# A Strassen identity for half of an output projection, with partial products accumulated on copied PSUM banks

## The chip, the cores and the metric

One core of one Trainium2 chip runs the whole kernel in one launch. The metric is the device time of one execution in microseconds (us); lower is better.

Engines in the profile: PE is the matrix engine (TensorE), PEld its weight loads, DVE is VectorE, ACT is ScalarE, POOL is GpSimd, SP issues most DMAs (289 of 348 in the profile before).

## The reference, cut to what matters

```python
xn = layernorm(x)                                  # 2048 tokens x 1024
q, k, v = split(xn @ wqkv)                         # 32 heads of 32
pq, pk = phi(q), phi(k)                            # phi(t) = (t+1 if t>0 else exp(t)) + 1e-6
kv, z  = einsum("bhsd,bhse->bhde", pk, v), sum(pk)
o = (pq @ kv) / (pq @ z + 1e-6)                    # linear attention
s = o @ wo                                         # <- the projection that is changed
g = silu((silu(xn @ w_gate) * (xn @ w_up)) @ w_down)
return x + s * g
```

Everything is bf16 at the borders; D = 1024, F = 3584.

## The kernel before

It has three stages. Stage 1 makes k, v and their products over all tokens. Stage 2 makes q, o and s for four blocks (0 to 3) of 512 tokens. Stage 3 is the gated MLP, already done with a Strassen identity; its weights are prepared ahead of time: ScalarE squares a weight piece to get a bound, VectorE scales it by a power of two, GpSimd forms four differences (T1 to T4). These "preparation steps" run inside stages 1 and 2.

Stage 2, cut:

```python
def emit_phi(work, t_ps, dst, W, in_place=False, act=False):
    if act:                                            # blocks 1 to 3
        nc.scalar.activation(out=e_t, in_=t_ps, func=ACT.Relu, scale=-1.0)
        nc.scalar.activation(out=e_t, in_=e_t, func=ACT.Exp, scale=-1.0)
        nc.scalar.activation(out=t_ps, in_=t_ps, func=ACT.Relu)
        nc.vector.scalar_tensor_tensor(out=dst, in0=e_t, scalar=EPS, in1=t_ps, ...)   # pqT
        return
    ...
def emit_ND(b, t, nd):            # numerator and denominator of one 128-token tile
    for g in range(G):            # 8 matmuls of 128x132 into three PSUM banks
        nc.tensor.matmul(nd[:, j, gi, :], lhsT=pqT[:, g, ttok], rhs=KVZ[:, g, :], ...)
    ...                           # VectorE: rden = 1/(den + EPS), then o_sb = num * rden
def emit_OT(b, t):                # o transposed by DMA; two oT buffers
    nc.sync.dma_start_transpose(out=oT_tiles[b][:, :, t*P:(t+1)*P], in_=o_blks[b][:, t, :])
def emit_S(b, t, cc):             # half a row tile of s: 8 matmuls of 128x512
    for c in range(G):
        nc.tensor.matmul(s_ps, lhsT=oT[:, c, ttok], rhs=wo_sb[:, c, cc*CW:(cc+1)*CW], ...)
    nc.scalar.copy(out=s_sb[...], in_=s_ps)
    ...
for b in range(NB):               # block b: q of b+1 mixed with s of b-1, nd of b in between
    q  = [q_item(b + 1, g) for g in range(G)] if b + 1 < NB else []
    sl = sh(b - 1, 0) + sh(b - 1, 1) if b > 0 else []
    ...                           # each nd_item also does one preparation step for b > 0
emit_Ssum(passes[0])              # VectorE: four 128x2048 sums S1 to S4 for stage 3
```

Of the kernel before, what the change touches and what calls it, by code (L numbers as in the profile page):

```python
# [21 lines left out]
def kernel(  # L22
# [41 lines left out]
    LEAD = 6  # L64
    NPK = 8

    wqkv_v = A_wqkv.rearrange("(dc p) n -> p dc n", p=P)
# [31 lines left out]
    nc.vector.memset(ones[:], 1.0)  # L99
    mask = persist.tile([P, P], FP32, name="mask")  # L100
    nc.vector.memset(mask[:], 0.0)
    for j in range(HPG):
        nc.vector.memset(mask[j * DH:(j + 1) * DH, j * DH:(j + 1) * DH], 1.0)
    sel = persist.tile([P, HPG], FP32, name="sel")
    nc.vector.memset(sel[:], 0.0)
# [13 lines left out]
    late = p12.enter_context(tc.tile_pool(name="late", bufs=1, reuse_waits="tile"))  # L119
    v_bufs = [late.tile([P, G, NDW], BF16, name=f"v_sb{k}") for k in range(2)]  # L120
    for k in range(2):
        nc.gpsimd.memset(v_bufs[k][:, :, P:P + 1], 1.0)
    KVZ = late.tile([P, G, NDW], BF16, name="KVZ")
# [3 lines left out]
    pk_drams = {}  # L127
    rc_all = persist.tile([P, 3 * NFG], FP32, name="rc_all")
    cs_all = persist.tile([P, 3 * NFG], FP32, name="cs_all")
    lam = persist.tile([P, NFG], FP32, name="lam")  # L130
    rcl = persist.tile([P, NFG], FP32, name="rcl")
    hsc = persist.tile([P, 3], FP32, name="hsc")
    chs, rch, hmx = hsc[:, 0:1], hsc[:, 1:2], hsc[:, 2:3]

    def emit_phi(work, t_ps, dst, W, in_place=False, act=False):
        e_t = work.tile([P, W], FP32, name="e_t", tag="e_t")
        if act:
            nc.scalar.activation(out=e_t[:], in_=t_ps, func=ACT.Relu, scale=-1.0)
            nc.scalar.activation(out=e_t[:], in_=e_t[:], func=ACT.Exp, scale=-1.0)
            nc.scalar.activation(out=t_ps, in_=t_ps, func=ACT.Relu)  # L140
            nc.vector.scalar_tensor_tensor(out=dst, in0=e_t[:], scalar=EPS, in1=t_ps,
                                           op0=ALU.add, op1=ALU.add)
            return
        nc.scalar.activation(out=e_t[:], in_=t_ps, func=ACT.Exp)
        if in_place:
            r = t_ps
            nc.vector.tensor_scalar(out=r, in0=t_ps, scalar1=0.0, scalar2=EPS, op0=ALU.max, op1=ALU.add)  # L147
        else:
            r_t = work.tile([P, W], FP32, name="r_t", tag="r_t")
            r = r_t[:]  # L150
            nc.scalar.activation(out=r, in_=t_ps, func=ACT.Relu)
            nc.vector.tensor_scalar(out=r, in0=r, scalar1=EPS, scalar2=None, op0=ALU.add)
        nc.vector.scalar_tensor_tensor(out=dst, in0=e_t[:], scalar=1.0, in1=r,  # L153
                                       op0=ALU.min, op1=ALU.add)
# [7 lines left out]

    def emit_Q(b, g):
        if b not in pqT_tiles:
            pqT_tiles[b] = blk12.tile([P, G, TB], BF16, name="pqT", tag="pqT")
        pqT = pqT_tiles[b]
        btok = slice(b * TB, (b + 1) * TB)
        q_ps = ps2.tile([P, TB], FP32, name="q_ps", tag="B2")
        for dc in range(DC):
            nc.tensor.matmul(q_ps[:], lhsT=wq_sb[:, dc, g * P:(g + 1) * P], rhs=xn_ap(dc, btok),  # L170
                             start=(dc == 0), stop=(dc == DC - 1))
        emit_phi(phiw, q_ps[:], pqT[:, g, :], TB, in_place=True, act=b > 0)

# [79 lines left out]

    def emit_st2(key, t, later=False):
        tot = stp.tile([P, 1], I32, name="tot", tag="tot")
        nc.vector.tensor_scalar(out=tot[:], in0=st_tiles.pop(key).bitcast(I32), scalar1=1, scalar2=0x3f800000,
                                op0=ALU.logical_shift_right, op1=ALU.bitwise_and)
        c = kcol(key)
        ri, ci = rc_all[:, c:c + 1].bitcast(I32), cs_all[:, c:c + 1].bitcast(I32)
        nc.vector.tensor_scalar(out=ri, in0=tot[:], scalar1=52 << 23, scalar2=None, op0=ALU.add)  # L260
        nc.vector.tensor_scalar(out=ci, in0=ri, scalar1=-1, scalar2=254 << 23, op0=ALU.mult, op1=ALU.add)
        if not later:
            emit_sc(key, t)
# [84 lines left out]
    with ExitStack() as p1:  # L348
# [4 lines left out]

        wkv_sb = wpool.tile([P, DC, 2 * D], BF16, name="wkv_sb")

        p1_man = ExitStack()
# [218 lines left out]
        emit_Bev(1, 3)  # L575
        emit_C(0)
        for i in range(2, NT):
            for c in range(NCH):
                if (i, c) != (2, 0):
                    emit_Bmm(i, c)  # L580
# [4 lines left out]
                emit_Bev(i, c)  # L585
                if c == 3 and i in (4, 6, 7):
                    prep(1)
# [15 lines left out]
        for j in range(NJ):  # L603
# [5 lines left out]
                                    in0=kvz_ps[:, j, 0:ng, P:P + 1].to_broadcast([P, ng, HPG]),  # L609
                                    in1=sel[:, None, :].to_broadcast([P, ng, HPG]), op=ALU.mult)  # L610
        for g in range(1, G):
            emit_Q(0, g)
            if g == 3:
                prep(1)
        p1_man.close()

    p2_man = ExitStack()
    p2_man.enter_context(tc.manual_schedule(engines={mybir.EngineType.SP}))
    s_sums = {}

    def emit_Ssum(p):
        x1 = xn_blk_tiles[2 * p]
# [4 lines left out]
        S4 = a21.bitcast(F16)  # L627
        nc.vector.tensor_tensor(out=S1[:], in0=a21, in1=a22, op=ALU.add)
        nc.vector.tensor_tensor(out=S2[:], in0=S1[:], in1=a11, op=ALU.subtract)
        nc.vector.tensor_tensor(out=S3[:], in0=a11, in1=a21, op=ALU.subtract)  # L630
        nc.vector.tensor_tensor(out=S4, in0=a12, in1=S2[:], op=ALU.subtract)
        s_sums[p] = (S1, S2, S3, S4, a22)

    with ExitStack() as p2:
        otp = p2.enter_context(tc.tile_pool(name="p2oT", bufs=2, reuse_waits="tile"))
        work = p2.enter_context(tc.tile_pool(name="p2work", bufs=4, reuse_waits="tile"))
        small = p2.enter_context(tc.tile_pool(name="p2small", bufs=6, reuse_waits="tile"))
        blk_es = ExitStack()
        blk = blk_es.enter_context(tc.tile_pool(name="p2blk", bufs=2, reuse_waits="tile"))
        oT_tiles = {}  # L640
# [3 lines left out]
        def emit_ND(b, t, nd):  # L644
            pqT = pqT_tiles[b]
            ttok = slice(t * P, (t + 1) * P)
            if b not in o_blks:
                o_blks[b] = blk.tile([P, TPB, D], BF16, name="o_blk", tag="o_blk")
            o_sb = o_blks[b][:, t, :]
            for g in range(G):  # L650
# [4 lines left out]
            for j0, j1, ng in ((0, NJ - 1, GPT), (NJ - 1, NJ, G - (NJ - 1) * GPT)):  # L655
                nc.vector.tensor_scalar(
                    out=rden[:, j0 * GPT:(j1 - 1) * GPT + ng, :].rearrange("p (j g) h -> p j g h", j=j1 - j0),
                    in0=nd[:, j0:j1, 0:ng, P:P + HPG], scalar1=EPS, scalar2=None, op0=ALU.add)
            nc.vector.reciprocal(out=rden[:, 0:G, :], in_=rden[:, 0:G, :])
# [9 lines left out]
        def emit_OT(b, t):  # L669
            if t == 0:  # L670
                oT_tiles[b] = otp.tile([P, G, TB], BF16, name="oT", tag="oT")
            nc.sync.dma_start_transpose(out=oT_tiles[b][:, :, t * P:(t + 1) * P], in_=o_blks[b][:, t, :])

        def emit_S(b, t, cc):
            oT = oT_tiles[b]
# [3 lines left out]
            s_sb = s_tiles[(b, t)]  # L679
            s_ps = ps2.tile([P, CW], FP32, name="s_ps", tag="B2")  # L680
            for c in range(G):
                mm = nc.tensor.matmul(s_ps[:], lhsT=oT[:, c, ttok], rhs=wo_sb[:, c, cc * CW:(cc + 1) * CW],  # L682
                                      start=(c == 0), stop=(c == G - 1))
                marks.setdefault(("S", b, t), mm)
            nc.scalar.copy(out=s_sb[:, cc * CW:(cc + 1) * CW], in_=s_ps[:])  # L685
            if cc == NCC - 1:
                r0 = b * TB + t * P
                nc.scalar.dma_start(out=s_dram[r0:r0 + P, :], in_=s_tiles.pop((b, t))[:])

        def q_item(b, g):  # L690
            return lambda: emit_Q(b, g)
# [4 lines left out]
        def nd_item(b, t):  # L696
            def f():
                raw, nd = psa_tile("nd")

                def nd_ot():  # L700
                    emit_ND(b, t, nd)
                    emit_OT(b, t)
                if b > 0 and (b < NB - 1 or t % 2 == 0):
                    stat_ps[0] = lambda: raw[:, 0, 511:512]
# [13 lines left out]

        for b in range(NB):
            q = [q_item(b + 1, g) for g in range(G)] if b + 1 < NB else []  # L720
            sl = sh(b - 1, 0) + sh(b - 1, 1) if b > 0 else []
            body = q[:2] + mix(q[2:], sl)
            at = (1, 4, 7, 10) if len(body) > 12 else ((1, 3, 5, 7) if b == 0 else (0, 2, 4, 6))
            for k, f in enumerate(body):
                f()
                if k in at:
                    nd_item(b, at.index(k))()
        b = NB - 1
        blk_es.close()
        blk12_es.close()  # L730
        sp = ctx.enter_context(tc.tile_pool(name="p3S", bufs=1, side="right", reuse_waits="tile"))
        emit_Ssum(passes[0])
        stat_ps[0] = lambda: psa_tile("st_ps3")[0][:, 0, 511:512]
        prep_flush()
        nc.scalar.preload_act_table(ACT.Silu)
        for f in sh(b, 0) + sh(b, 1):
            f()
    p2_man.close()
# [511 lines left out]
```

## Time and profile before

| | before |
|---|---|
| median of the first three runs | 764.8 us (764.25 to 765.98) |
| first q matmul, first matmul of stage 3, first of the last down projections | 127.83, 249.69, 748.80 us |
| stage 1 (first k·v product to first q), stage 2, stage 3 up to that point | 102.63, 121.86, 499.11 us |

The marks are start times of the first matmul of that kind in the timeline. First the busy times on the page (busy us, share of the span, instructions):

```profile
PE 752.7 (99%) x3731; PEld 350.4 (46%) x3731; DVE 543.6 (71%) x1026; ACT 348.3 (46%) x479; POOL 269.1 (35%) x382
```

TensorE bounds the kernel: only 9 us of 762.1 are not matmul time. Second, stage 2 in the table of stretches; after the stretch's length come busy us of PE, PEld, DVE, ACT and POOL, each with its instruction count, the granted PE clock, the DMA share and GB/s.

```profile
127.00:166.00 39.00, 36.62 (x206) 17.56 (x205) 29.30 (x65) 26.62 (x46) 20.94 (x18) 1.00 0.65 191
166.00:210.00 44.00, 44.00 (x246) 21.51 (x245) 29.46 (x82) 38.86 (x62) 26.86 (x24) 1.00 0.98 269
210.00:262.00 52.00, 52.00 (x275) 24.90 (x274) 29.40 (x62) 24.48 (x39) 19.43 (x17) 1.00 0.89 278
```

From 166 us on PE is full. VectorE has room throughout (29 of 39, 29 of 44, 29 of 52), ScalarE except in the middle stretch (39 of 44), and GpSimd is busy for half of the time (67 of 135 us in the sum of that table). This invites moving work off PE. Third, what PE waited for (total us, times, longest), as far as it concerns stage 2:

```profile
PE nd L652 <- DVE o_blk L663: 1.7, 2, 1.2
...
PE nd L652 <- DVE pqT L153: 0.4, 1, 0.4
...
PE q_ps L170 <- DVE pqT L153: 0.2, 1, 0.2
```

Together 2.3 us. In the timeline the sums S1 to S4 of stage 3 take 2.15, 2.06, 1.21 and 1.23 us. These are the sums S1 to S4 of stage 3 in the timeline (start, us, engine, line, operation, out<-in, shapes), with the GpSimd instruction that ran at the same time:

```profile
236.30 2.15 DVE L628 TENSOR_TENSOR S<-xnT 128x2048 f16<-128x2048 bf16 x1
...
237.33 2.13 POOL L283 TENSOR_TENSOR w_sb<-w_sb 128x512 f16<-128x512 bf16 x1
...
238.49 2.06 DVE L629 TENSOR_TENSOR S<-S,xnT 128x2048 f16<-128x2048 f16 x1
...
240.47 1.21 DVE L630 TENSOR_TENSOR S<-xnT 128x2048 f16<-128x2048 bf16 x1
...
241.72 1.23 DVE L631 TENSOR_TENSOR xnT<-xnT,S 128x2048 f16<-128x2048 bf16 x1
```

Four instructions of one size and kind take 2.15, 2.06, 1.21 and 1.23 us. The two slow ones ran while GpSimd was at work, and the GpSimd instruction next to them took 2.13 instead of its usual 1.15 us.

### The profile page before, as it was taken

Reading aid. Unit: us, or ns where it says so; the run is one execution under the profiler, and the core shown is the slowest. Engines: PE = TensorE matmul, PEld = TensorE weight load, DVE = VectorE, ACT = ScalarE, POOL = GpSimd, SP = SyncE. Lnnn points to the kernel's source line nnn. Section 1 sums busy time; section 2 is a strip of 40 time slices with the busy share of each in tenths; the row PEclk is TensorE's granted clock in tenths of the full one; section 3 lists DMA queues with packets and bytes.
Section 4 is the critical chain, followed back from the end, with each engine's and each line's share of the span. In section 5 each row is a group of like instructions: output and inputs, shape, how many; then the busy total and the mean of one; then the engine's idle time right before and its main releaser. Section 6 shows DMA issues by size and latency. Waiting matters only on the chain.

```text
span 762.1 us, 10455 instructions
## 1 busy us (share of the span) xinstructions
PE 752.7 (99%) x3731; PEld 350.4 (46%) x3731; DVE 543.6 (71%) x1026; ACT 348.3 (46%) x479; POOL 269.1 (35%) x382
## 2 busy tenths in 40 slices
PE   8999999999999999999999999999999999999997
PEld 3444444444444444444444444444444444444444
DVE  7788676876656588888889885358676767787335
ACT  4545777688853566666448411132323222211022
POOL 0577699708563255868655000110000000200000
PEclk9999999999999999999999999999999999999999
DMA  9986799669889769897887237398654445530824
GB/s 315 302 151 125 204 298 319 248 139 286 238 263 263 250 231 308 290 359 289 314 310 281 86 86 260 116 355 329 228 190 177 166 165 170 170 144 15 281 81 136
DMA packets 105908, 170.29 MB, mean 223 GB/s; under 512 B 34688, under 2 KB 82176, under 8 KB 95232
## 3 DMA queue, kind: packets, MB, share of 16 engines
q1 hardware_dynamic: 99280, 143.81, 59.9%
q0 software_dynamic: 3984, 21.24, 7.0%
q10 hardware_dynamic: 2592, 4.59, 1.8%
q8 instruction: 29, 0.48, 0.3%
q14 instruction: 23, 0.19, 0.1%
HBM read 111.67 MB, written 50.59 MB: 213 GB/s over the span
## 4 chain that ended last, share of the span: by engine, by line
PE 94%; DVE 2%; DMA 1%; ACT 1%; issue 1%; SPq 0%; ACTq 0%; DVEq 0%
PE zw L754 25%; PE kv_ps L508 14%; PE xb L754 13%; PE dzw L939 12%; PE s_ps L682 7%; PE yb L754 6%; PE dx L939 6%; PE q_ps L170 4%; PE dy L939 3%; DMA wkv_sb<-in_A_wqkv_dram 1%; PE kvz L530 1%; PE nd L652 1%; PE df L939 1%; DVE pqT L153 1%; DVE q_ps L147 1%
## 5 line engine op out<-in xcount | busy, mean ns | idle before, releaser
L754 PEld LDWEIGHTS <-w_sb 128*128 128x128 f16 (+1 forms) x1568 | 152.2, 98 | 182.9 <-issue 0.2
L508 PE MATMUL kv_ps<-wkv_sb,xnT 128*128 128x512 bf16 x512 | 113.7, 379 | 1.5 <-DMA wkv_sb<-in_A_wqkv_dram 0.8
L754 PE MATMUL xb<-xnT,w_sb 128*128 128x512 bf16 x448 | 115.0, 379 | 0.0
L754 PE MATMUL zw<-xnT,w_sb 128*128 128x512 bf16 x448 | 105.8, 379 | 0.0
L754 PE MATMUL zw<-S,w_sb 128*128 128x512 f16 x448 | 105.8, 379 | 0.0
L280 POOL TENSOR_TENSOR w_sb<-w_sb 128x512 f16<-128x512 bf16 x42 | 49.2, 1172 | 118.5 <-ACT s_sb L685 31.4
L247 ACT ACTIVATE w_sb<-w_sb 128x2048 bf16<-128x2048 bf16 x42 | 79.9, 1902 | 8.4 <-DMA w_sb<-in_B_w_up_dram 5.6
L939 PE MATMUL dx<-w_sb,hT 128*128 128x512 bf16 x210 | 79.6, 379 | 0.0
L508 PEld LDWEIGHTS <-xnT 128*128 128x128 bf16 x512 | 48.5, 97 | 57.1 <-issue 1.5
L939 PEld LDWEIGHTS <-hT 128*128 128x128 bf16 (+1 forms) x462 | 45.2, 98 | 51.7
L170 PE MATMUL q_ps<-xnT,wq_sb 128*128 128x512 bf16 x256 | 58.5, 379 | 0.2 <-DVE pqT L153 0.2
L939 PE MATMUL dzw<-w_sb,hT 128*128 128x512 f16 x196 | 58.3, 379 | 0.0
L682 PE MATMUL s_ps<-wo_sb,oT 128*128 128x512 bf16 x256 | 57.8, 379 | 0.0
L754 PE MATMUL yb<-S,w_sb 128*128 128x512 f16 x224 | 57.4, 378 | 0.0
L782 DVE SCALAR_TENSOR_TENSOR s<-yb,rc_all,s 128x512 f32<-128x512 f32 x42 | 31.5, 749 | 35.1 <-ACT s L781 35.0
L830 ACT ACTIVATE sg<-cg 128x1024 bf16<-128x1024 f32 x28 | 29.6, 1057 | 57.4 <-DVE cg L823 57.4
L823 DVE SCALAR_TENSOR_TENSOR cg<-zw,rc_all,s 128x1024 f32<-128x1024 f32 x28 | 35.9, 1284 | 25.9 <-PE zw L754 14.0
L283 POOL TENSOR_TENSOR w_sb<-w_sb 128x512 f16<-128x512 bf16 x42 | 50.8, 1210 | 0.0
L281 POOL TENSOR_TENSOR w_sb<-w_sb 128x512 f16<-128x512 bf16 x42 | 49.5, 1178 | 3.3
L282 POOL TENSOR_TENSOR w_sb<-w_sb 128x512 f16<-128x512 bf16 x42 | 50.3, 1198 | 0.0
L879 POOL TENSOR_TENSOR hs<-hT 128x512 f16<-128x512 bf16 x2 | 2.5, 1254 | 132.6 <-ACT sg L830 132.6
L913 POOL DMA_DIRECT2D out_dram<-io x16 | 8.7, 542 | 101.9 <-DVE io L912 101.6
(152 smaller groups left out, 1082.0 us busy)
## 6 DMA issues: line engine op xcount, KB each, us to landing
w_sb<-pk_g SPq DMA_DIRECT2D x27, 1024.0 KB, 5.6
pk_g<-w_sb SPq DMA_DIRECT2D x14, 1024.0 KB, 5.2
w_sb<-wd SPq DMA_DIRECT2D x14, 1024.0 KB, 5.0
w_sb<-pk_u SPq DMA_DIRECT2D x14, 1024.0 KB, 4.9
pk_u<-w_sb POOLq DMA_DIRECT2D x13, 1024.0 KB, 6.1
w_sb<-wd SPq DMA_DIRECT2D x14, 768.0 KB, 5.9
w_sb<-in_B_w_gate_dram SPq DMA_DIRECT2D x14, 512.0 KB, 6.4
w_sb<-in_B_w_down_dram SPq DMA_DIRECT2D x28, 256.0 KB, 3.9
```

The source lines that it names most:

```text
L170: nc.tensor.matmul(q_ps[:], lhsT=wq_sb[:, dc, g * P:(g + 1) * P], rhs=xn_ap(dc, btok), start=(dc == 0), stop=(dc == DC - 1))
L247: nc.scalar.activation(out=junk, in_=raw_view(key, t), func=ACT.Square, accum_out=asum[:])
L280: nc.gpsimd.tensor_tensor(out=T1, in0=b12, in1=b11, op=ALU.subtract)
L281: nc.gpsimd.tensor_tensor(out=T2, in0=b22, in1=T1, op=ALU.subtract)
L282: nc.gpsimd.tensor_tensor(out=T3, in0=b22, in1=b12, op=ALU.subtract)
L283: nc.gpsimd.tensor_tensor(out=T4, in0=b21, in1=T2, op=ALU.subtract)
L508: mm = nc.tensor.matmul(kv_ps[:], lhsT=xn_ap(dc, tok), rhs=wkv_sb[:, dc, c * CW:(c + 1) * CW], start=(dc == 0), stop=(dc == DC - 1))
L682: mm = nc.tensor.matmul(s_ps[:], lhsT=oT[:, c, ttok], rhs=wo_sb[:, c, cc * CW:(cc + 1) * CW], start=(c == 0), stop=(c == G - 1))
L754: mm = nc.tensor.matmul(out, lhsT=lhs(k), rhs=rhs(k), start=(first and k == 0), stop=(k == HK - 1), skip_group_check=True)
L782: nc.vector.scalar_tensor_tensor(out=s2[:], in0=y_[:], scalar=rc, in1=s1[:], op0=ALU.mult, op1=ALU.add)
L823: nc.vector.scalar_tensor_tensor(out=d12, in0=zw[:], scalar=rc, in1=s2[:, None, :].to_broadcast([P, 2, TB]), op0=ALU.mult, op1=ALU.add)
L939: nc.tensor.matmul(out, lhsT=lhs, rhs=rhs, start=first, stop=lastk, skip_group_check=True)
```

## The change

The intent: in blocks 2 and 3 replace 8 products of half tiles by 7. A unit takes two token tiles (t1, t2) of one block; o's contraction is cut in halves (a11, a12; a21, a22 for t2) and wo in quarters. With S1 = a21+a22, S2 = S1-a11, S3 = a11-a21, S4 = a12-S2, T1 = b12-b11, T2 = b22-T1, T3 = b22-b12, T4 = b21-T2, seven products of four matmuls each give all four quarters of s. Products that share a partial result accumulate in PSUM: ScalarE copies a bank (X to Y, Y to Z) and the next product accumulates on the copy. The sums are fp16, so powers of two are measured: one for wo (four Squares, wo scaled in place), one for o (from KVZ, folded into 1/den), and taken out again in the copies with the 128x1 factor `s_sc`. The change also lets the last pqT instruction go behind nd's evacuation on VectorE (`phi_late`), moves the two last preparation steps, adds one in token tile 5 in exchange, gives three of block 0's q groups the ScalarE form of phi, and puts S3 of stage 3 on GpSimd.

```diff
+    phi_late = []                       # pqT instruction emitted after the next nd evacuation
+            phi_late.append(lambda: nc.vector.scalar_tensor_tensor(out=dst, in0=e_t[:], ...))
 ...
+        def wo_stat(q):   nc.scalar.activation(..., in_=wo_q(q), func=ACT.Square, accum_out=wo_st[:, q:q+1])
+        def wo_scale(q):  nc.vector.tensor_scalar(out=wo_q(q), in0=wo_q(q), scalar1=cs_all[:, CWO:CWO+1], ...)
 ...                                     # in token tiles 6 to 9 and 10 to 13 of stage 1
+            if g == 5:                  # end of stage 1: bound on o
+                nc.vector.tensor_reduce(out=zr[:], in_=KVZ[:, :, P:P + HPG], ...)
+                nc.vector.reciprocal(out=zr[:], in_=zr[:])
+                nc.vector.tensor_tensor(out=ojunk[:], in0=KVZ[:, :, 0:P], in1=zr[...].to_broadcast(...), op=ALU.mult)
+                nc.scalar.activation(out=ojunk[:], in_=ojunk[:], func=ACT.Square, accum_out=ost[:])
+    def o_pow2():
+        nc.tensor.matmul(ps, lhsT=ones[:], rhs=ost[:], ...)          # one column
+        emit_pow2(ps, CWO + 1)
+        nc.vector.tensor_tensor(out=s_sc[:], in0=rc_all[:, CWO:CWO+1], in1=rc_all[:, CWO+1:CWO+2], op=ALU.mult)
 ...
+        for o_, a_, b_ in (...):        # To: four 128x2048 differences of wo
+            nc.gpsimd.tensor_tensor(out=o_, in0=a_, in1=b_, op=ALU.subtract)
+        def s_unit(b, u):
+            def sums():                 # four 128x512 instructions on VectorE
+                nc.vector.tensor_tensor(out=so[:, 0], in0=a21, in1=a22, op=ALU.add)
+                ...
+            def x():  mmk(X, a11, b11, True);  nc.scalar.copy(out=Y[:], in_=X[:])
+            def w():  mmk(W, so[:, 0], To[0], True);  ...            # copy to SBUF, times s_sc
+            def y():  mmk(Y, so[:, 1], To[1], False); nc.scalar.copy(out=Z[:], in_=Y[:]); ...
+            def x2(): mmk(X, a12, b21, False); ...                   # quarter 11 of s
+            def z():  mmk(Z, so[:, 2], To[2], False); ...            # VectorE: Z*s_sc + w
+            def z2(): mmk(Z, a22, To[3], False); ...
+            def w2(): mmk(W, S4, b22, False); ...                    # VectorE: W*s_sc + s2
 ...
-        for b in range(NB): ...
+        run(q[:2] + mix(q[2:], sh(1, 0)), (1, 4, 7, 10), 2, (0, 2, 1, 3))
+        emit_S(1, 2, 0); emit_S(1, 2, 1)
+        u["sums"](); nds[0](); u["x"](); u["w"](); emit_S(1, 3, 0, fx[4]); nds[1]()
+        units[1]["sums"](); u["y"](); u["x2"](); emit_S(1, 3, 1, fx[4]); nds[2](); u["z"]()
 ...                                     # three more units, sums of stage 3 between them (S3 on GpSimd)
```

## The prediction

> **What bounds the kernel now.** TensorE: the page gives PE 752.7 of 762.1 us busy, clock 1.00; the table of stretches shows 100% from 20 to 127 and 165 to 500 us. Q work and the o/wo projection lie between 127 and 250 us; there PE's list of waits holds 2.3 us: nd on o_blk (VectorE) 1.7, nd on pqT 0.4, q_ps on pqT 0.2. Eight 128x512 matmuls take 1.73 us in the timeline, 0.216 each[...].
>
> **Removed.** Blocks 2 and 3 need 128 s_ps matmuls; four units of 7 products of 4 make 112: minus 16 x 0.216 = 3.45 us, all on the critical path. Five one-column matmuls (0.03 us spacing) add 0.15. Deferring the last pqT instruction lets nd's evacuation go first on VectorE: most of the 1.7 us of nd waits should go.
>
> **Added off PE.**
> - ScalarE: four Squares of wo (2.1 us each, from the w_sb Squares) in token tiles 6 to 9, where it is 5.1 to 5.6 busy of each 7 to 8 us. Three kv_ps banks absorb about 3.5 us of lag: 0 to 0.5 us of PE wait.
> - GpSimd: four To differences, about 4.7 us each (4 x 1.17), in the hole at 145 to 165 us (3.3 busy of 20): free.
> - VectorE: four sums per unit, about 2 us (a quarter of the S rows: 2.15, 2.06, 1.21, 1.23), two combines of 0.75; a unit lasts 6.05 us on PE.
> - ScalarE per unit: six copies of 0.6. A copied bank is ready about 0.95 us after its product; a product takes 0.86, and nearly everywhere two stand between.
>
> **New PE waits expected.**
> - o's power of two: KVZ sum, reciprocal, 128x1024 product, Square, then a one-column matmul after Q(1,0). From the timeline this chain ends near 146 us; PE arrives near 144.5: 1 to 2 us. Then the first nd waits about 1 us for pqT (before: 0.4).
> - Block 2's loop is shorter (8 Q, 4 S, four prep steps): ScalarE needs 8x1.8 + 4x0.6 + 4x2.1 = 25 us against PE's 23, so block 3's first nd waits about 1 us for pqT.
> - Last unit, copies one product apart: 0.4 us.
>
> **Sum.** -3.45 +0.15 -1.75 +2.5 (o scale, first nd) +1 +0.4 +0.3 (kv_ps) = -0.85; if the order was well tuned, new waits vanish: -4.5 to -5. I take -2.2.
>
> Predicted 762.6 us, 80% range 760.2 to 765.2. Faster by over 2%: 0.005; within 2%: 0.985; slower: 0.01.
>
> **What would show it.** Block 2 and 3 projection matmuls: 112 instead of 128, at 0.216 us. The stretch from the first q_ps to the next stage's first yb (127.8 to 249.9 us, 122.1 us) shortens by about the difference in total. PE's list of waits: o_blk gone or small; new entries for the one-column matmul on ScalarE's accumulator, nd on pqT, under 0.5 us on copies; kv_ps on ScalarE under 0.5 us at 55 to 90 us.
>
> **What would make it wrong.** (1) The o-scale chain ends before PE asks: 759 to 760. (2) o's last transposes (5 to 7 us to land here) come late: VectorE stands in its sums and evacuations behind it stall PE by several us. (3) The next stage starts late because its weights collide with those transposes. (4) ScalarE's saturation stalls kv_ps by over a microsecond.

Two figures are estimates, and the prediction does not say from what: the 3.5 us that three kv_ps banks absorb agree with two groups of eight matmuls at 1.73 us each, and for the 0.95 us until a copied bank is ready, the trace of the change shows 0.99 us in the second unit (its product is done at 238.83 us, the copy at 239.82).

## The result, and the profile after

| | before | after |
|---|---|---|
| median | 764.5 us (764.06 to 765.98) | 778.1 us (777.74 to 778.49, 4 runs) |
| first q, first of stage 3, first of the last down projections | 127.83, 249.69, 748.80 | 130.33, 261.78, 762.71 |
| stages 1, 2, 3 | 102.63, 121.86, 499.11 us | 104.32, 131.45, 500.93 us |

The ratio is 1.0175 (95% interval 1.0157 to 1.0192). A ratio is the mean time of one kernel's fast runs over the mean of the other's in the same rounds, so it is not quite the ratio of the medians. The result matches the reference: e1 and e7 below do the same arithmetic and were checked. The range of the prediction, 760.2 to 765.2, is missed by 13 us: the kernel is slower by 1.75%. That it came out within 2%, which the prediction gave 0.985, is no credit to its argument, since the sign is wrong.

The busy time says that the intended saving took place:

```profile
PE 749.4 (97%) x3651; PEld 349.8 (45%) x3720; DVE 570.3 (74%) x1060; ACT 365.8 (47%) x503; POOL 292.3 (38%) x387
```

PE has 3.3 us less work, and the span is 13.9 us longer. Stage 2 lost 9.6 us, stage 1 1.7, stage 3 1.8; the first k·v product came 0.8 us later, which varies from profile to profile (25.06 to 26.59 us over all of them). The same stretches as before:

```profile
127.00:166.00 39.00, 31.87 (x168) 15.11 (x170) 31.10 (x66) 26.88 (x46) 38.53 (x25) 1.00 0.66 213
166.00:210.00 44.00, 43.74 (x246) 21.80 (x250) 30.46 (x81) 39.58 (x63) 25.53 (x21) 1.00 0.88 240
210.00:262.00 52.00, 44.72 (x232) 21.10 (x236) 40.94 (x79) 27.88 (x45) 23.11 (x17) 0.97 0.82 234
```

Two holes: 127 to 166 and 210 to 262 us. In the first GpSimd went from 20.9 to 38.5 of 39 us; in the second VectorE went from 29.4 to 40.9, and the granted clock fell to 0.97. (The second stretch holds 12 us of stage 3 before and none after, so only part of that rise is due to the units.) What PE waited for:

```profile
PE fx L795 <- DVE s_sb L832: 4.4, 2, 3.3
PE nd L723 <- DVE o_blk L735: 2.9, 1, 2.9
PE nd L723 <- DVE wq_sb L735: 2.6, 1, 2.6
...
PE st_ps L675 <- ACT ojunk L667: 1.5, 1, 1.5
PE kv_ps L523 <- DVE pk_sb L160: 1.2, 2, 1.0
...
PE q_ps L180 <- DVE pqT L160: 1.1, 2, 0.9
PE nd L723 <- DVE pqT L148: 0.5, 1, 0.5
```

Two names need a word: `fx` are the five PSUM banks of the units, and `wq_sb` in block 3 stands for o and for the units' sums, which are written into the buffer of wq once q is done. The units' copies, which the prediction worried about, do not appear. The largest lines name VectorE. The timeline of VectorE, GpSimd and PE (chosen lines) shows why. First the 2.9 us wait at block 0's second nd:

```profile
152.62 4.06 POOL L767 TENSOR_TENSOR To_sb<-wo_sb 128x2048 f16<-128x2048 bf16 x1
...
154.23 2.47 DVE L677 TENSOR_TENSOR s_sc<-rc_all 128x1 f32<-128x1 f32 x1
...
156.62 0.36 DVE L727 TENSOR_SCALAR rden<-nd,rc_all 128x24 f32<-128x24 f32 x2
156.75 4.06 POOL L767 TENSOR_TENSOR To_sb<-wo_sb,To_sb 128x2048 f16<-128x2048 bf16 x1
...
158.81 0.64 PE L723 MATMUL nd<-KVZ,pqT 128*128 128x132 bf16 x8 [2.87 <-DVE o_blk L735]
```

A product of two 128x1 columns takes 2.47 us and ends when GpSimd's To difference ends (152.62 + 4.06 = 156.68); the next difference starts then. The evacuation behind it, which PE needs, is late by as much. Second, the sums of the first unit:

```profile
222.88 0.63 PE L723 MATMUL nd<-KVZ,pqT 128*128 128x132 bf16 x8
...
223.09 0.46 DVE L788 TENSOR_TENSOR wq_sb<-oT 128x512 f16<-128x512 bf16 x1
...
223.34 1.22 POOL L293 TENSOR_TENSOR w_sb<-w_sb 128x512 f16<-128x512 bf16 x1
...
223.64 1.20 DVE L789 TENSOR_TENSOR wq_sb<-wq_sb,oT 128x512 f16<-128x512 f16 x1
...
224.52 1.33 POOL L294 TENSOR_TENSOR w_sb<-w_sb 128x512 f16<-128x512 bf16 x1
224.76 1.37 DVE L790 TENSOR_TENSOR wq_sb<-oT 128x512 f16<-128x512 bf16 x1
...
225.81 1.33 POOL L295 TENSOR_TENSOR w_sb<-w_sb 128x512 f16<-128x512 bf16 x1
226.17 1.26 DVE L791 TENSOR_TENSOR oT<-oT,wq_sb 128x512 f16<-128x512 bf16 x1
...
227.35 0.36 DVE L727 TENSOR_SCALAR rden<-nd,rc_all 128x24 f32<-128x24 f32 x2
...
229.55 0.64 PE L723 MATMUL nd<-KVZ,pqT 128*128 128x132 bf16 x8 [2.58 <-DVE wq_sb L735]
```

Each of the last three sums ends 0.28 or 0.29 us after the GpSimd difference that ran beside it. A sum that takes 0.42 us alone (232.30 to 233.96 in the same profile) takes 1.20 to 1.37 us, so the four last 4.3 us and the evacuation at 227.35 starts late; PE waits 2.58 us. Third, the last unit:

```profile
249.00 1.26 DVE L791 TENSOR_TENSOR oT<-oT,wq_sb 128x512 f16<-128x512 bf16 x1
...
249.94 1.33 POOL L295 TENSOR_TENSOR w_sb<-w_sb 128x512 f16<-128x512 bf16 x1
...
250.18 2.17 DVE L690 TENSOR_TENSOR S<-xnT 128x2048 f16<-128x2048 bf16 x1
...
252.27 0.74 DVE L832 SCALAR_TENSOR_TENSOR s_sb<-fx,s_sc,s 128x512 bf16<-128x512 f32 x1
...
253.06 1.86 PE L795 MATMUL fx<-To_sb,wq_sb 128*128 128x512 f16 x4 [3.27 <-DVE s_sb L832]
...
254.72 1.67 PE L795 MATMUL fx<-To_sb,oT 128*128 128x512 f16 x4
...
256.22 1.03 PE L795 MATMUL fx<-To_sb,wq_sb 128*128 128x512 f16 x4
```

The same contention in unit 3's sums and in the first 128x2048 sum of stage 3 (2.17 us, alone 1.22) delays a combine; PE waits 3.27 us. Then something else shows: the next two groups of four matmuls take 1.86 and 1.67 instead of 1.03 us. The granted clock had dropped: it was 0.62 in the stretch from 253 to 257 us and 1.00 in the next four us. What makes it drop was not shown; other executions had the same wait without it (the last section lists them). Half speed lasted from 253.06 to about 256.2, 3.1 us, and cost (1.86 + 1.67) - 2 x 1.03 = 1.5 us.

What the contention depends on, the traces show only in part. The sums (two SBUF inputs) stretch from 0.42 to 1.2–1.4 us, and GpSimd's differences beside them from 1.15 to 1.22–1.33, while o's evacuation (128x384, one input in PSUM) takes 1.35 us (three instructions) whether GpSimd runs (157.41 us) or not (228.14 us). Instructions with one tensor in SBUF can be stretched too: the scaling of a 128x2048 weight piece by a column takes 0.75 us in the change where GpSimd is idle, and the four scalings of wo in stage 1, all beside GpSimd, take 1.32 to 1.64 us.

### The profile page after: what moved, and what is told of

The parts are those of the page before. It is cut to its first block, busy times and chain, and to the rows that moved or that the text cites. A ratio compares the mean times of both kernels' runs of the same rounds, so it can differ in the third digit from the quotient of the medians.

```text
span 776.0 us, 10448 instructions
## 1 busy us (share of the span) xinstructions
PE 749.4 (97%) x3651; PEld 349.8 (45%) x3720; DVE 570.3 (74%) x1060; ACT 365.8 (47%) x503; POOL 292.3 (38%) x387
## 4 chain that ended last, share of the span: by engine, by line
PE 65%; DMA 3%; DVE 2%; issue 1%; ACT 1%; SPq 0%; DVEq 0%; ACTq 0%
PE zw L946 24%; PE xb L946 12%; PE dzw L1131 12%; PE yb L946 6%; PE dx L1131 6%; PE dy L1131 3%; DMA w_sb<-in_B_w_up_dram 2%; PE fx L795 1%; PE df L1131 1%; DMA s_dram<-s_sb 1%; DMA oT<-wq_sb 1%; PE dz L1131 0%; DVE S L690 0%; ACT w_sb L1328 0%; PE fx L754 0%
## 5 line engine op out<-in xcount | busy, mean ns | idle before, releaser
L946 PE MATMUL xb<-xnT,w_sb 128*128 128x512 bf16 x421 | 113.4, 379 | 2.6 <-ACT sg L1021 1.1
L946 PE MATMUL zw<-xnT,w_sb 128*128 128x512 bf16 (+1 forms) x447 | 105.8, 379 | 0.1
L292 POOL TENSOR_TENSOR w_sb<-w_sb 128x512 f16<-128x512 bf16 x42 | 51.2, 1218 | 98.3 <-DVE w_sb L280 34.4
L1131 PE MATMUL dx<-w_sb,hT 128*128 128x512 bf16 x202 | 76.6, 379 | 0.3
L1131 PE MATMUL dzw<-w_sb,hT 128*128 128x512 f16 (+1 forms) x190 | 57.0, 379 | 0.0
L293 POOL TENSOR_TENSOR w_sb<-w_sb 128x512 f16<-128x512 bf16 x42 | 50.6, 1205 | 3.3
L295 POOL TENSOR_TENSOR w_sb<-w_sb 128x512 f16<-128x512 bf16 x42 | 50.7, 1207 | 0.0
L294 POOL TENSOR_TENSOR w_sb<-w_sb 128x512 f16<-128x512 bf16 x42 | 50.2, 1195 | 0.0
L973 ACT ACTIVATE s<-xb,rcl 128x512 f32<-128x512 f32 x14 | 9.6, 687 | 65.0 <-PE xb L946 65.0
```

The source lines that it names most:

```text
L292: nc.gpsimd.tensor_tensor(out=T1, in0=b12, in1=b11, op=ALU.subtract)
L293: nc.gpsimd.tensor_tensor(out=T2, in0=b22, in1=T1, op=ALU.subtract)
L294: nc.gpsimd.tensor_tensor(out=T3, in0=b22, in1=b12, op=ALU.subtract)
L295: nc.gpsimd.tensor_tensor(out=T4, in0=b21, in1=T2, op=ALU.subtract)
L946: mm = nc.tensor.matmul(out, lhsT=lhs(k), rhs=rhs(k), start=(first and k == 0), stop=(k == HK - 1), skip_group_check=True)
L1131: nc.tensor.matmul(out, lhsT=lhs, rhs=rhs, start=first, stop=lastk, skip_group_check=True)
```

## The experiments

Theory P: the change puts VectorE instructions with two SBUF inputs beside GpSimd, where they take longer (0.42 us against 1.20 to 1.37), and VectorE's delay reaches PE (waits of 2.6 to 3.3 us). Rivals: the units themselves (copies, banks), the power-of-two measurements, and late transposes of o. All kernels are correct unless said otherwise. Medians come with the range over all their runs.

### e1: the 128x1 product on ScalarE

```diff
-        nc.vector.tensor_tensor(out=s_sc[:], in0=rc_all[:, CWO:CWO+1], in1=rc_all[:, CWO+1:CWO+2], op=ALU.mult)
+        nc.scalar.activation(out=s_sc[:], in_=rc_all[:, CWO:CWO+1], func=ACT.Copy, scale=rc_all[:, CWO+1:CWO+2])
```

> [...] The one-column product s_sc took 2.47 us on VectorE because a 4.06 us To difference ran on GpSimd, and the second nd waited 2.87 us behind it. Here only that product moves to ScalarE, later. P: that nd wait falls from 2.87 to about 0.4 us and the total by 2.0 to 2.7 us against the change. Rival Q (VectorE's queue is just too long there, one small instruction less changes little): the nd wait stays above 2 us and the total moves by under 0.5 us.

Measured: 775.8 us (774.95 to 777.64), ratio to before 1.0153 (1.0138 to 1.0169), 2.3 us below the change. The evacuation follows at once (compare 154.23 to 156.62 above):

```profile
153.33 0.15 DVE L270 TENSOR_SCALAR cs_all<-rc_all 128x1 int32<-128x1 int32 x1
153.40 0.37 DVE L726 TENSOR_SCALAR rden<-nd,rc_all 128x24 f32<-128x24 f32 x2
```

The wait for o_blk fell from 2.9 to 0.5 us. One tiny instruction cost 2.3 us because it stood behind a 4 us GpSimd instruction. The 2.3 us is the difference of the medians (the ranges just do not overlap). The one profile of e1 does not show it: its stage 2 took 132.10 us against 131.45, because half speed followed the nd wait of 2.56 us as well, and lasted longer after the one of 3.27 us (clock 0.84 at 220 to 230 us and 0.66 at 250 to 260).

### e2: the last preparation step of block 2 moved behind block 3's first nd; the final flush behind the last unit's sums

```diff
-                if 0 < b < NB - 1:
+                if (0 < b < NB - 1 and (b, t) != (2, 3)) or (b, t) == (3, 0):
-                    'x w new Ssum -z2 sums p y -w2 x2 z p'          # prep_flush() inside Ssum
+                    'x w new Ssum -z2 sums p y -w2 x2 z p flush'
```

> Same work on every engine, two preparation steps moved: the last one of block 2 goes to the first nd of block 3 (behind the sums of the first unit on VectorE), and the flush behind the last unit's sums, so that GpSimd's four differences no longer run under those sums. Theory P: the four sums of the first and of the last unit take about 1.7 us instead of 4.2, the nd wait on wq_sb (2.58) and the product's wait of 3.27 us go, also the throttled matmuls after it: total 5 to 8 us less than the change. Rival Q (VectorE has too much work between its deadlines, whoever else runs): VectorE's work is unchanged, so the waits stay within 1 us of what they were. Rival D (the transposes of o land late): the waits stay, with the sums beginning after a DMA wait.

Measured: 773.3 us (771.37 to 774.62), ratio 1.0109 (1.0092 to 1.0126): -4.9 us, just under the range. The sums of units 0 and 3 now take 0.42 us each, and the waits of 2.6 and 3.3 us are gone. But the moved GpSimd work now meets two sums of unit 1 (1.26 and 1.37 us), stage 3's S3 on GpSimd (4.06 us) meets the first of unit 2 (2.32 us), and a new wait of 1.2 us stands at a later nd. The collision moved; part of it came back.

### e3: wo not scaled

```diff
-                if c == 1 and i in WO_ST: wo_stat(...)
-                if c == 3 and i == WO_ST[-1]: wo_pow2()
-                if c == 3 and i in WO_SC: wo_scale(...)
+                if c == 3 and i == WO_ST[-1]: nc.gpsimd.memset(rc_all[:, CWO:CWO+1], 1.0)
```

> The four Squares of wo, their power of two and the four scalings of wo are left out (the factor is set to 1; the result should stay right). Theory S: they cost the first stage about 1.5 us (four VectorE scalings of 1.3 to 1.6 us in tiles 10 to 13 and the GpSimd waits that they cause): start of the first q_ps moves from 130.3 to about 128.5 us, total 1.5 to 2 us less than the change. Rival: the extra preparation step in tile 5 makes GpSimd run late and ScalarE wait for it in tile 15 (0.98 us wait of kv_ps), and the start varies by 0.8 us by itself: under 0.7 us gained.

Measured: 776.7 us (775.85 to 778.72), ratio 1.0166 (1.0148 to 1.0183): -1.4 us, with ranges that overlap. In the profile stage 1 is back at 102.66 us (-1.66). Its stage 2 took 133.29 us, 1.8 more, with half speed after the waits of 2.87 and 2.57 us, so this profile shows no gain in total. PE's wait on pk_sb (1.2 us, two waits) is in the profile of every kernel that scales wo and in none of the others with this change (e3, c2, c4, c6, c7, c8). The prediction had put +0.3 here.

### e4 and e4b: only the deferred pqT instruction, in the kernel before

```diff
+    phi_late = []
-            nc.vector.scalar_tensor_tensor(out=dst, in0=e_t[:], scalar=EPS, in1=t_ps, ...)
+            phi_late.append(lambda: nc.vector.scalar_tensor_tensor(out=dst, in0=e_t[:], scalar=EPS, in1=t_ps, ...))
             ...
                     nd_item(b, at.index(k))()
+                phi_flush()
```

> The kernel before with one part of the change alone: the last VectorE instruction of phi is issued behind the nd evacuation. As the prediction had it: nd's waits on o_blk (1.7 us) go, total 1 to 1.8 us below before. Rival: nothing gained, since the pqT instruction now comes later and nd or q_ps waits for it: within 0.5 us of before.

Measured: 762.8 us (762.09 to 763.83), ratio 0.9981 (0.9966 to 0.9996). Both waits for o_blk are gone and stage 2 takes 119.70 instead of 121.86 us. In the rounds of the last versions:

> The kernel before with only the deferred pqT instruction, a second time, in the same rounds as the three repaired versions, so that they can be compared with it: 762.8 us as before (761.9 to 763.5), ratio 0.998 to the kernel before. If Strassen's 16 matmuls (3.45 us) come through where nothing waits, c6 and c7 lie 1.5 to 3 us below it; if the support work eats them, they lie at or above it.

Measured: 764.0 us (762.58 to 764.30), ratio 0.9988 (0.9976 to 1.0). By the ratios the two are closer than by the medians: -1.5 and -0.9 us. In both profiles stage 3 took 501.3 us against 499.1 in the one profile of before, so most of the 2.2 us is given back there; what gives it back was not settled (see the end of the discussion).

### e5: the GpSimd differences of the two last preparation steps left out (wrong result)

```diff
-            emit_T(*k3, later=True)
+            if not (k3[0][1] == "w" and k3[0][2] >= 6):
+                emit_T(*k3, later=True)
```

> The change with nothing moved on any engine, but the four GpSimd differences of the two last preparations left out (two weight tiles are wrong, so the result is wrong on purpose). Theory P[...]: the first and last unit's sums on VectorE fall to about 0.42 us each from up to 1.4; the nd wait of 2.58 and the product's wait of 3.27 us go or fall under 0.8; total 5 to 8 us less than the change. Rival Q' (what helped in the reordered run was that VectorE's own scaling instructions were moved from before the deadlines): they are still in their place here, so the two waits stay above 2 us and the total within 1.5 us of the change.

Measured: 771.0 us (770.0 to 771.8), ratio 1.0087 (1.0072 to 1.0102): -7.2 us. The output is wrong (relative error 0.42), as intended. The waits of 2.6 and 3.3 us are gone, with every VectorE instruction left in place. The sums of units 0 and 3 take 0.41 to 0.43 us each; one of unit 0:

```profile
224.44 0.42 DVE L790 TENSOR_TENSOR wq_sb<-wq_sb,oT 128x512 f16<-128x512 f16 x1
```

So it is GpSimd's overlap, not the number of VectorE instructions, that made them. With e1 this makes 9.5 of the 13.6 us, if the two add, as e8 suggests; no run has exactly these two together.

### e6: the units undone, their support kept

```diff
-        ... units, fx banks, sums ...
+        q = qs(3)
+        run(q[:2] + mix(q[2:], sh(1, 0) + sh(1, 1)), (1, 4, 7, 10), 2)
+        run(sh(2, 0) + sh(2, 1), (0, 2, 4, 6), 3)      # plain 128 matmuls
+        ...
```

> The change with the Strassen units undone: blocks 2 and 3 are projected by the plain 128 matmuls in the order of before; the scaling of wo and o, the To differences on GpSimd, the deferred instruction and the preparation in tile 5 stay. If the supporting work outside the units costs what its waits show (first stage 1.7, o's scale and the first nds about 5, minus 2.3 of old waits, plus up to 2 in the last stage): 768 to 772 us, so the units themselves account for 6 to 10 us of the loss, not for a gain. Rival (the loss is in the supporting work, the units do gain their 3.4 us): 779 us or more.

Measured: 771.6 us (771.12 to 772.33), ratio 1.0094 (1.0077 to 1.011). So as placed in the change, the units cost 6.5 us more than the 128 matmuls that they replace, as expected (6 to 10), and the support (powers of two, To differences, with the gain of the deferred pqT in it) costs 7 us over before. That includes the o_blk wait of 2.9 us that e1 removes.

### e7: block 1's last projection steps early

```diff
         nds[0]()
+        emit_S(1, 3, 0, fx[4]); emit_S(1, 3, 1, fx[2])
+        nds[1]()
         u["x"]()
+        units[1]["sums"]()
         u["w"]()
-        emit_S(1, 3, 0, fx[4]); nds[1](); units[1]["sums"]()
         u["y"]()
-        u["x2"](); emit_S(1, 3, 1, fx[4]); nds[2](); u["z"]()
+        nds[2](); u["x2"](); u["z"]()
```

In the change block 3's four transposes were all issued together at 233.68 us, because their buffer was still read by those steps. It was suspected that this holds VectorE up.

> The changed kernel with one thing moved: the last two plain projection steps of block 1 (token tile 3) go in front of block 3's second nd and before the first unit, so that the last reader of block 1's transposed o is done early and block 3's transposes can start one by one as each piece of o is evacuated. Same instructions, same number. Theory T (the transposes of block 3 stand behind the buffer of block 1's o and land late, which makes VectorE wait for oT in the sums and PE behind it): block 3's four transposes are issued one after the other from about 228 us instead of all at 233.7, VectorE's wait of 1.1 us on oT goes, and the time falls by 1 to 2 us, to 776 to 777. Rival (the transposes are hidden; what PE waits for is VectorE's contention with GpSimd alone): the transposes move but the wait of 2.6 us at block 3's second nd and the one of 3.3 us at 253 us stay, and the time stays within 0.7 us of 778.1.

Measured: 779.1 us (777.86 to 781.39), ratio 1.0186 (1.0161 to 1.0211), the same as the change. The transposes started at 230.21 us, VectorE's wait of 1.1 us on them went, and the waits of 2.6 and 3.3 us stayed. The rival held: late transposes, failure case (2) of the prediction, were not the cause of these waits. The 1.1 us did not come free, though: the sum that had waited now started 2.0 instead of 3.2 us after stage 3's S3 on GpSimd and took 2.32 instead of 1.12 us.

### e8: three repairs at once (e1, e2, e7)

> The changed kernel with three repairs at once, each moved before or now by itself: the 128x1 product on ScalarE (-2.3 us alone), the last preparation step of block 2 moved behind block 3's first nd (-4.9 us alone), and block 1's last projection steps early (as in the run beside this one). If the causes are separate waits they add up: 778.1 - 2.3 - 4.9 - (0 to 2) = 769 to 771. If they share a wait (the repaired collision only moves to the next place where GpSimd and VectorE meet), it stays at 772 or above.

Measured: 769.1 us (767.69 to 770.56), ratio 1.0051 (1.0027 to 1.0075): -9.1 us, more than e1 and e2 give alone (7.2). The repairs are separate waits and add up. The surplus goes with the clock: it is 0.999 to 1.0 in e8's runs, 0.993 to 0.997 in e1's and 0.997 to 1.0 in e2's.

### c1 to c4: towards a version without the waits

c1 is the change with the sums kept apart from GpSimd: o's power of two is measured in block 1 and used from block 2 on, block 2's last preparation step and the final one are done in block 1, S3 goes to VectorE and the 128x1 product to ScalarE. c2 is c1 without wo's scaling.

```diff
-               lambda: nc.gpsimd.tensor_tensor(out=S3[:], in0=a11, in1=a21, op=ALU.subtract),
+               lambda: nc.vector.tensor_tensor(out=S3[:], in0=a11, in1=a21, op=ALU.subtract),
-                if 0 < b < NB - 1:
+                if 0 < b < NB - 1 and (b, t) != (2, 3):
 ...
+        run(body[:12] + [o_chain] + body[12:13] + [xprep] + body[13:15] + [xo] + body[15:] + [xprep], (1, 4, 7, 10), 1)
```

> The change rearranged, same arithmetic: o's scale is measured in block 1 and used only from block 2 on, block 0's phi is as before, all GpSimd differences end before the first unit's sums (two preparation steps more in block 1, none after block 2's third), the layer's third sum is back on VectorE, s_sc on ScalarE. If the collisions[...] and the o chain are the cause in this stage: P2 (first q_ps to first yb) from 131.5 to about 117 to 119 us against 121.9 before, waits of products on sums under 1 us in all. Total 760 to 764, as the first stage keeps its 1.7 us and the last may give back up to 2. Rival (units too dense for VectorE and ScalarE even without GpSimd): P2 above 122, total above 766.

> As the rearranged version, and wo is not scaled (factor 1): first stage back to 102.6 us from 104.3, total 1.3 to 1.8 us less than the rearranged version: 758.5 to 762.5, the best of all. Rival (last stage bound by its weight loads, a start that is 1.6 us earlier is given back there): equal to the rearranged version within 0.5 us.

Measured: c1 767.8 us (764.68 to 769.47), ratio 1.0041 (1.0014 to 1.0068); c2 767.3 us (764.59 to 768.94), ratio 1.0036 (1.0008 to 1.0063). In c1 no wait on the units' sums or their combines is left, but PE waits 2.2 us for pqT and 0.7 for a statistic in block 1, and stage 2 took 120.92 us where 117 to 119 was expected; c2 also waits 1.6 and 0.6 us for combines. So the theory held for the collisions, and the time was missed. The runs of one kernel differ by 4 to 5 us. In c2's profile half speed followed the wait of 2.19 us for pqT; in c1's, at full clock throughout, it did not follow the same wait. c3 adds e7's order, statistics columns in other banks and a fifth buffer for the rows of s; c4 is c3 without wo's scaling.

```diff
-        stat_ps[0] = lambda: ps2.tile([P, 1], FP32, name="st_ps2", tag="B2")[:]
+        stat_ps[0] = lambda: psa_tile("st_x")[0][:, 0, 511:512]
-        work = p2.enter_context(tc.tile_pool(name="p2work", bufs=4, ...))
+        work = p2.enter_context(tc.tile_pool(name="p2work", bufs=5, ...))
```

> The moved version (o's scale measured in block 1 and used from block 2 on, both late preparation steps in block 1[...]) with three more repairs: block 1's last projection early, the columns for the statistics in the nd banks instead of the ring of the five banks (there PE waited 2.2 us for pqT and 0.7 for a statistic), and five instead of four buffers for the rows of s. Theory: what made c1 vary from 764.7 to 769.5 us between runs is the landing of transposes and stores under buffers that are too few; so the time comes to 760 to 763 us and the runs agree within 1.5 us. Rival: the variation has another cause (the granted clock, or the next stage's weights); then it stays 764 to 769 and varies as before.

> As the run before it, but wo is not scaled (factor 1, no Squares, no scaling on VectorE; this holds for data whose weights and o are within fp16's range as here, and gives up the safeguard). The scaling cost 1.7 us in the first stage in the change (measured by itself: -1.4 us). Theory: 1.4 to 1.7 us below the run before it, 758.5 to 761.5 us. Rival (the start of the stage given back in a later wait, as seen when only the scale was left out): within 0.7 us of the run before it.

Measured: c3 767.2 us (766.68 to 770.47), ratio 1.0041 (1.0016 to 1.0065); c4 766.0 us (765.03 to 767.56), ratio 1.0012 (0.9993 to 1.0031). Against the expectation: buffers were not what varied. c4's timeline shows one wait and its price (PE only):

```profile
184.14 5.34 PE L744 MATMUL s_ps<-wo_sb,oT 128*128 128x512 bf16 x23
192.31 0.16 PE L664 MATMUL st_x<-ost,ones 128*128 128x1 bf16 x1 [2.83 <-ACT s_sb L882]
...
192.74 5.02 PE L180 MATMUL q_ps<-xnT,wq_sb 128*128 128x512 bf16 x16
```

PE waits 2.83 us for ScalarE's Square in front of the one-column matmul, and then 16 matmuls start over 4.86 us (192.74 to 197.60) instead of 3.45. In the stretch from 190 to 200 us the granted clock is 0.83. A wait of under 3 us cost over 4.

### c5, c6, c7: the measurement of o back at the end of stage 1, then without any scaling

c5 is c3 with the KVZ sum, product and Square where the change has them, only the one-column matmul late; c6 is c5 without wo's scaling; c7 is c6 without o's measurement too (factor 1 on both, right for this data, without the safeguard for larger values).

```diff
-        run(body[:13] + [xprep, o_chain] + body[13:] + [xo, xprep], ...)
+        run(body[:13] + [xprep] + body[13:] + [xo, xprep], ...)          # c5, c6
+        run(body[:13] + [xprep] + body[13:] + [xprep], ...)              # c7
```

> c3 with the measurement of o's power of two back at the end of the first stage (as in the change), its one-column matmul alone staying at the end of block 1; c3 had the measurement in front of that matmul, and PE waited 2.9 us for ScalarE's Square there, after which the granted clock was 0.83 in that stretch of 10 us. Theory: that wait and the half-rate matmuls after it are what c3 lost: 2.9 + about 1.6 us, so the time comes to 762 to 763.5 us, with no wait on the one-column matmul over 0.3 us and a clock of 1.00 at 190 to 200 us. Rival: ScalarE is full in block 1 with the extra preparation steps and the wait moves to q_ps or to nd on pqT there; then 765.5 to 767 us.

> The same with factor 1 for wo (no Squares, no scaling). Theory: 1.2 to 1.7 us below the run before it, 760.5 to 762 us, so below before (764.5) by about 3 and near before with only the deferred pqT instruction (762.8). Rival: within 0.7 us of the run before it.

> As the run before it, without o's power of two as well (factor 1 on both; right for this data, gives up the safeguard). It bounds what the safeguard for o still costs once nothing waits for it. Theory: nothing is left of that cost: within 0.6 us of the run before it. Rival (VectorE at the end of the first stage is still late by the 2 us of the chain): 1 to 1.5 us below it.

Measured: c5 766.7 us (764.34 to 767.72), ratio 1.0026 (1.0012 to 1.0039); c6 764.3 us (763.0 to 767.18), 0.9995 (0.9983 to 1.0007); c7 761.2 us (759.53 to 761.59), 0.9953 (0.9941 to 0.9965). For c5 neither side of the expectation was right: the wait in block 1 went and the clock there is 1.00, but it came back earlier, at the first nd of block 0 (c6, PE only):

```profile
147.81 0.51 PE L719 MATMUL nd<-KVZ,pqT 128*128 128x132 bf16 x6
150.24 0.23 PE L719 MATMUL nd<-KVZ,pqT 128*128 128x132 bf16 x1 [1.92 <-DVE pqT L160]
151.14 0.29 PE L719 MATMUL nd<-KVZ,pqT 128*128 128x132 bf16 x1 [0.67 <-DVE pqT L148]
151.22 5.23 PE L180 MATMUL q_ps<-xnT,wq_sb 128*128 128x512 bf16 x16
...
156.76 3.61 PE L180 MATMUL q_ps<-xnT,wq_sb 128*128 128x512 bf16 x16
```

The same place in c7 (PE only):

```profile
146.81 0.57 PE L706 MATMUL nd<-KVZ,pqT 128*128 128x132 bf16 x7
147.82 0.23 PE L706 MATMUL nd<-KVZ,pqT 128*128 128x132 bf16 x1 [0.45 <-DVE pqT L160]
147.89 3.62 PE L180 MATMUL q_ps<-xnT,wq_sb 128*128 128x512 bf16 x16
```

With the measurement, VectorE and ScalarE deliver pqT late: 1.92 + 0.67 us of waits, then 16 matmuls in 5.23 instead of 3.61 us. Without it, 0.45 us. That is 2.1 + 1.6 = 3.7 us, beside 3.2 us between the medians of c6 and c7 and 5.1 between the stage 2 of their profiles (122.56 and 117.47; c6's profile is of its slowest run, 767.18 us). In c7 the sums are free of GpSimd and the units cost nothing: no wait on them is in its list, and all but the first sum of unit 0 take 0.42 us.

### c8 and c9: o's measurement in block 1, in front; then with wo's scaling

```diff
-        run(body[:13] + [xprep] + body[13:] + [xprep], (1, 4, 7, 10), 1)
+        run(body[:3] + [o_chain] + body[3:13] + [xprep] + body[13:] + [xo, xprep], (1, 5, 8, 11), 1)
```

> The fastest version so far (no power of two at all, 761.2 us) with o's power of two measured again, but placed where nothing waits for it: the chain KVZ sum, reciprocal, product, Square behind the third Q group of block 1, its one-column matmul at the end of block 1, use from block 2 on. At the end of the first stage the same chain cost PE 2.6 us of waits for pqT and 1.6 us of half-rate matmuls (3.2 us between the medians). Theory: the place was the cost, not the work; 761 to 762.3 us, no wait over 0.6 us between 140 and 215 us, clock 1.00 there. Rival: ScalarE is full in block 1 (9.1 to 9.4 us of each 10 without the chain) and 1.3 us more of it comes out as a wait for pqT: 762.5 to 764.5 us.

> The run before it with wo's power of two as well (four Squares in token tiles 6 to 9, four scalings on VectorE in 10 to 13), so the whole safeguard of the change. Alone this cost 1.4 us of the change's time and 1.65 us of its first stage, and no repair of it is tried here. Theory: 1.4 to 2.5 us above the run before it, 762.5 to 764.5 us, so at the kernel before or up to 0.3% below it: the safeguard eats what Strassen gains over the deferred pqT alone. Rival: the later start is made up by a wait that then ends earlier: within 0.7 us of the run before it.

Measured: c8 765.7 us (764.53 to 767.48), ratio 1.0019 (1.0006 to 1.0032); c9 765.3 us (764.37 to 766.88), 1.0013 (1.0 to 1.0025). For c8 the rival held, and more: ScalarE is nearly full in block 1 (8.7 to 9.4 of each 10 us from 170 to 200; in c7, without the chain, 9.1 to 9.5), the chain comes out as waits of 1.4 and 0.9 us on statistics, and the time is 4.5 us above c7. The profile names VectorE's small instructions for these waits, so that ScalarE is behind them is not shown. For c9 the rival held too: stage 1 took 1.6 us more (104.26 against 102.67) and the time did not.

The six runs of c8 show what varied since c1: three have a granted clock of 0.999 to 1.0 and took 764.5 to 764.8 us, three have 0.997 and took 766.6 to 767.5. c1 (764.7 at 1.0, 766.9 at 0.999; 768.7 and 769.5 at 0.998 and 0.997) and c6 (763.0 and 763.6 at 1.0, 764.0 at 0.999; 765.5 and 767.2 at 0.998) are the same kind, though c6 has one run of 764.7 at 0.997. The clock is not all of it: c4's six runs, all at 0.996 or 0.997, range from 765.0 to 767.6. The profiles show what a lower clock is made of: the same wait is followed by half speed in some executions and not in others (the last section lists them). That c8's slow runs split off at such a wait is likely but not shown, since only a run at 1.0 was profiled; what decides it is open.

## Why the prediction was wrong

**The saving was right.** 112 matmuls stand for 128, and PE's busy time fell by 3.3 us. c7 against e4b, which differ by the units and what they need, in the same rounds: 761.2 against 764.0 us. So 2.8 of the predicted 3.45 us come through where nothing waits (roughly: c7 also places two preparation steps and the last plain projections otherwise than e4b); c6, which still measures o, is at 764.3 and keeps none of it. The deferred pqT instruction was predicted at -1.75; e4 measured -1.8 and, again, -0.2 against before in its rounds.

**The step that failed** is the costing of the work off PE by itself, "GpSimd: four To differences ... in the hole at 145 to 165 us ...: free" and "VectorE: four sums per unit, about 2 us". The differences took 4.06 us each, and the four sums take 1.7 us alone. Neither size was far off. But each takes longer while the other is at such an instruction: the sums 1.20 to 1.37 us instead of 0.42, the differences beside them 1.22 to 1.33 instead of 1.15. In the change this made 4.3 us of sums out of 1.7 and 2.47 us out of a 128x1 product, always ahead of an evacuation or a combine that PE needed. The sum of the prediction (-0.85 us) has no term for it. Measured: 2.3 us (e1) and 7.2 us (e5); in the profile of the change about 1.5 of it is the clock after the long wait, which other executions of the same wait did not pay. The warning was in hand: the sums of 2.15, 2.06, 1.21 and 1.23 us were averaged as "about 2 us" per unit, though two of them were twice the others and GpSimd's own instruction beside them had doubled.

| term | predicted | measured |
|---|---|---|
| 16 matmuls fewer | -3.45 us | -2.8 us (c7 against e4b) |
| deferred pqT | -1.75 | -1.8 (e4), -0.2 (e4b); by the ratios -1.5, -0.9 |
| o's power of two and the first nd | +2.5 | 1.5 and 0.5 of waits in the change; +3.2 (c6 against c7), up to half of it at half clock |
| wo's power of two | +0.3 | +1.4 (e3); +0.6, +1.2, +2.3 (c1, c3, c5 against c2, c4, c6); -0.4 (c9 against c8) |
| pqT at block 3's first nd | +1 | not seen in the list of waits |
| copies in the last unit | +0.4 | not seen: the waits on fx name VectorE's combines |
| VectorE against GpSimd | none | +9.5 (e1 and e5), 1.5 of it the clock |

The measured terms of the table do not add up to 13.6 exactly, since each comes from another pair of kernels and a wait removed at one place can return at another.

**The failure cases.** Case (2) named the right symptom, "VectorE stands in its sums and evacuations behind it stall PE by several us", with the wrong cause: e7 brought the transposes forward and nothing changed. Case (4), kv_ps waits of over a microsecond, came true in size (1.2 us in two waits), but the trace names VectorE's pk_sb, at 112 and 128 us, not ScalarE's saturation at 55 to 90 us. It comes with wo's scalings on VectorE (see e3). Case (3), a late stage 3, is possible and open.

**What stays open.** Stage 3 takes 499.1 to 501.6 us in the profiles, without an order that follows the change: 499.1 in before and c3, 499.4 in c1, 501.3 in e4, c7 and c8, 500.9 in the change. It goes with one transfer: ScalarE's longest wait for a piece of the up weights is 2.6 us in before, 2.9 in c3 and 4.6 in c1, but 5.8 in the change, 6.4 in e4 and 6.5 in c7, and those three have a wait of PE for ScalarE's silu of 1.1 to 1.2 us. Why that piece lands late in some kernels could not be told from single profiles. It takes up to 2 us from a gain made in stage 2. Also open: a place for o's measurement at which it is free. Three places were tried and each cost 3 us or more against c7.

**The versions.** Only c7 is below both kernels (761.2 us, 0.5% below before), and it gives up the safeguard that the change's scaling provides. With the whole safeguard, c9 at 765.3 us is no better than before. Deferring the pqT instruction alone (e4) costs nothing and is worth 0.1 to 0.2%.

## What to carry to other kernels

When work moves from a bound engine to idle ones, cost each moved VectorE instruction that reads SBUF and not PSUM twice: alone, and beside whatever GpSimd runs then (here 0.42 us and 1.20 to 1.37 us for a 128x512 sum); if the same instruction has two durations in the trace before, find out which neighbour makes the difference before using either. A delay on VectorE costs what stands behind it in its order (here waits of PE of 2.6 to 3.3 us), so keep such instructions away from evacuations that the matrix engine waits for. And count a PE wait of about 2 to 3 us in an otherwise full stream at about half as much again, because in these runs the clock often dropped after it: that cost 1.5 us after a wait of 3.27 us in the change, 1.4 after 2.83 in c4 and 1.6 after 1.92 + 0.67 in c6.

## What the traces showed of the clock and of the two engines

- Half speed followed single waits of 3.26 or 3.27 us (the change, e1, e7), 2.83 to 2.87 (e2, e3, e5, e6, e7, c3, c4), 2.56 or 2.57 (e1, e3) and 2.19 us (c2), and 1.92 + 0.67 us with one matmul between (c6). It did not follow the same waits of 3.27 us in e3, 2.87 in the change, 2.57 and 2.58 in e7 and the change, and 2.19 in c1. The mean clock of the executions where it followed was 0.993 to 0.998, and 1.0 in c1's. So the same wait does not always cost the clock. What decides is open.
- 3.1 us at half speed cost 1.5 us in the change, and 16 matmuls took 5.23 instead of 3.61 us in c6. Runs of one kernel can differ by this: 764.5 to 764.8 us at a clock of 0.999 to 1.0 and 766.6 to 767.5 at 0.997 (c8).
- VectorE beside GpSimd shows in the profile as a longer instruction, not as a wait. A 128x512 sum went from 0.42 to 1.20–1.37 us, a 128x2048 one from 1.22 to 2.1–2.2, a 128x1 product to 2.47, and GpSimd's 128x512 difference from 1.15 to 1.22–1.33, in places to 2.13.
- Two of a unit's seven products accumulate on a non-zero copy by ScalarE, and every kernel with units that was checked (except e5) is correct.
